# Wq loaded in twelve pieces of 16 rows instead of two pieces of 128, and x in one piece instead of three

## The chip, the core and the metric

The kernel runs on one core of a Trainium2 chip. The core has a matrix engine (TensorE, in the profile PE, with PEld for its weight loads), a vector engine (VectorE, DVE), a scalar engine (ScalarE, ACT), a general engine (GpSimd, POOL) and a synchronisation engine (SyncE, SP), which here only issues transfers. Transfers between the chip's memory (HBM) and the on-chip memory of 128 partitions (SBUF) run on 16 DMA engines; SP and ACT each have a queue on them. The metric is the device time of one execution in microseconds (us), as a median of several runs. A profile is the record of one execution; its span runs from the first to the last instruction of the program and is a little shorter than the device time of that execution.

## What is computed

One step of decoding for 8 sequences (B = 8, one token each): a layer norm of x, attention over a window of the last 2048 positions of a cache, and a gate from a small feed-forward unit. All arrays are bf16; D = 512, 32 query heads that share 8 key and value heads, head size 128, F = 1792.

```python
xn = layernorm(x)                                  # x: [8, 1, 512]
q = (xn @ wq).reshape(8, 1, 32, 128)               # wq: [512, 4096]
k, v = k_cache[:, :, -2048:, :], v_cache[:, :, -2048:, :]   # [8, 8, 2048, 128]; each serves 4 query heads
p = softmax(q . k * 128 ** -0.5)
s = (p . v).reshape(8, 1, 4096) @ wo               # wo: [4096, 512]
h = sigmoid(xn @ w_gate) * (xn @ w_up)             # [512, 1792] each
g = silu(h @ w_down)                               # [1792, 512]
out = x + s * g
```

Of 81 MB that are read, the windows of the K and V caches are 32 MB each in binary units, Wq and Wo 4 MB each, and the three matrices of the feed-forward unit 1.75 MB each.

## The kernel before

The order of the work is written out by hand. All large loads go through one function, `load` (its issue is L116), which issues on SP's queue; the transfers of that queue run in the order of their issues. The list `loads` fixes this order: after Wq the eight K tiles and sixteen V tiles, interleaved by their due slots, then the matrices of the feed-forward unit and Wo at the end.

Wq, the K tiles, and the weights of the end share a ring of three buffers (`kring`, 32 KB or less in each partition); the V tiles have a ring of four. Wq takes the first buffer of `kring`, the first two K tiles the other two. The third K tile can be issued only when the q projection has read Wq (the entry `(4, 0)` in `k_order`, released behind `q_projection`). `issue_loads` runs after each slot of the main loop and issues what has become possible.

In SBUF, row p of `wq_sb` holds rows 4p to 4p + 3 of Wq (the index `kt` is 0 to 3), that is 16,384 elements or 32 KB of contiguous memory. Before, two loads of 128 rows bring it: the first 4096 columns (kt = 0, 8 KB in each partition), then the other 12,288 (24 KB in each).

x is [8, 512]. It comes through ACT's queue (L126) in three pieces of columns 0 to 255, 256 to 383 and 384 to 511. L244 to L257 on VectorE and ScalarE normalise it, L267 on TensorE transposes it, L285 writes `xnT_sb`. The q projection (L405) then runs 32 matmuls: for each of two groups of heads and each kt, four matmuls with 32 columns of output partitions each. Every matmul reads all 128 partitions of `wq_sb` for its kt. `q_out` copies the result and lays it out in `qz_sb` (L419 to L436).

The main loop goes by slots. In each, VectorE transposes a quarter of the columns of a half K tile in place (`k_turn`, L464), TensorE makes scores four slots later (`qk`, L479), and later in the loop come the softmax, its transposes and the products with V (`pv`, L609). Behind the loop stand the last products, the feed-forward unit's output, and the product with Wo (L723), which takes Wo's six loads as they land. L734 and L736 combine, L738 stores.

In the compiled program a transfer takes one of eight completion semaphores in turn. An issue that reuses a semaphore waits until the transfer that had it eight places before has landed. Before the change, x and Wq take five (three and two); after it thirteen (one and twelve), so that the later transfers keep the same semaphores.

Of the kernel before, what the change touches and what calls it, by code (L numbers as in the profile page):

```python
# [10 lines left out]
def kernel(  # L11
# [13 lines left out]
    nc = tc.nc  # L25
    P = 128
# [53 lines left out]
    NSUM = 4  # L80
    NCOL = 2
    DC = D // NCOL
    WQ0 = 4096

    bf16 = mybir.dt.bfloat16
    f32 = mybir.dt.float32
# [26 lines left out]
    def load(dst, src, q=None):  # L113
        if q is None:
            q = nc.sync
        q.dma_start(out=dst, in_=src)  # L116
# [5 lines left out]
        return vring.tile(shape, bf16, name=name, tag="vring", align_bytes=ALIGN)  # L122

    x_bf = work.tile([B, D], bf16, name="x_bf")
    for c0, c1 in ((0, 2), (2, 3), (3, 4)):
        nc.scalar.dma_start(  # L126
            out=x_bf[:, P * c0 : P * c1],
            in_=A_x.flatten_outer_dims()[:, P * c0 : P * c1],
        )

    wq_sb = k_tile([P, KT, Hq * Dh], "wq_sb")
    wq_rows = A_wq.rearrange("(p kt) n -> p (kt n)", kt=KT)
    wq_flat = wq_sb[:].rearrange("p kt n -> p (kt n)")
    load(wq_flat[:, :WQ0], wq_rows[:, :WQ0])
    load(wq_flat[:, WQ0:], wq_rows[:, WQ0:])

    k_tiles = {}
    v_tiles = {}
# [77 lines left out]
    def issue_loads():  # L216
# [36 lines left out]
        out=rstd[:], in_=mv[:, 1:2], func=AF.Sqrt, bias=eps_t[:], scale=1.0  # L253
# [4 lines left out]
        out=xn_bf[:],  # L258
# [7 lines left out]
    for kt in range(KT):  # L266
        nc.tensor.transpose(  # L267
            out=xnT_ps[:, kt, :], in_=xn_bf[:B, kt::KT], identity=ident[:B, :B]
        )
    x2_ps = psum1.tile([NCOL * 32, DC], f32, name="x2_ps", tag="misc")  # L270
    for c in range(NCOL):
# [18 lines left out]
        out=HR[:],  # L290
        in_=ident[:].rearrange("m (h q r) -> m h r q", q=NQ, r=rep),
# [6 lines left out]
        out=Qm[:],  # L298
        in_=ident[:].rearrange("m (h q r) -> m q h r", q=NQ, r=rep),
# [6 lines left out]
        out=Hm[:],  # L306
        in_=ident[:].rearrange("p (a gl) -> p gl a", gl=GL),
# [6 lines left out]
    for j in range(GL):  # L314
        for gg in range(NG):
            g = NG * gg + j // 2
            nc.gpsimd.tensor_copy(
                out=spread[:, gg, j % 2, :, j], in_=ident[:, 32 * g : 32 * g + PP]
# [5 lines left out]
        out=rows_of[:],  # L324
        in_=ident[:].rearrange("p (a m) -> p m a", m=w),
# [5 lines left out]
        out=Sel[:], in_=rows_of[:].rearrange("p (g c r) -> p c g r", g=GL, c=NCH)  # L331
# [5 lines left out]
    for gg in range(NG):  # L337
        rows = slice(32 * gg, 32 * (gg + 1))
        cols = slice(NE * GL * rep * gg, NE * GL * rep * (gg + 1))
        for e in range(NE):  # L340
            nc.gpsimd.tensor_copy(
                out=pick[rows, e, cols].rearrange("p (h d) -> p h d", d=NE)[:, :, e],
                in_=ident[rows, 32 * gg : 32 * gg + GL * rep],
# [325 lines left out]
    for t in range(PV_LAG + NSLOT):  # L669
# [18 lines left out]
        if u >= NJ and u % NJ == 0:  # L688
            i = u // NJ - 1
# [47 lines left out]
    for c in range(NCOL):  # L737
        queues[c].dma_start(  # L738
            out=out.flatten_outer_dims()[:, DC * c : DC * (c + 1)],
            in_=y_bf[32 * c : 32 * c + B, :],  # L740
# [31 lines left out]
```

## Time and profile before

| | us |
|---|---|
| median of 3 runs | 197.32 (197.01 to 197.46) |
| the profiled execution | 197.11 |
| its span | 195.3 |
| TensorE busy (matmuls) | 102.8 |
| VectorE busy | 105.4 |
| ScalarE busy | 30.8 |
| GpSimd busy | 4.6 |
| mean rate of transfer over the span | 415 GB/s |

The page of the profile names the busy time of each engine, shows the span in 40 slices (a digit is the busy share in tenths), lists the transfer queues and their packets, and follows the chain of work that ended last back from the end. Further views are: the chain in order of time; a timeline of instructions; a table of stretches, with each engine's busy time and count, the clock granted to TensorE, the mean busy share of the DMA engines, and the rate in GB/s; and the instructions of one line of code, with the shortest, median and longest of them. A short stretch counts a packet of a transfer in the stretch where it begins, so its rate and share can lie above or below the true one.

### The profile page before, as it was taken

What the parts mean: (1) busy time and instruction counts of PE and PEld (TensorE: products, weight loads), DVE (VectorE), ACT (ScalarE), POOL (GpSimd) and SP (SyncE); (2) the same over time, 40 slices, a digit from 0 to 9 for tenths busy, and PEclk for the clock granted to TensorE, in tenths of its full rate; (3) what the DMA queues carried; (4) which work ended last, traced back from release to release, by engine and by line L of the source; (5) the groups of instructions that cost most, each with busy time, mean ns of one, the idle gap of its engine ahead of it and who ended that gap; (6) DMA issues with size and microseconds to landing.
All of it is one profiled execution on the core that took longest, in us unless ns stands there. A gap on an engine that the chain in (4) does not pass through costs nothing.

```text
span 195.3 us, 1888 instructions
## 1 busy us (share of the span) xinstructions
PE 102.8 (53%) x750; PEld 36.2 (19%) x750; DVE 105.4 (54%) x149; ACT 30.8 (16%) x69; POOL 4.6 (2%) x25
## 2 busy tenths in 40 slices
PE   0062014434323248403695989858943893577763
PEld 0020001101000012100121222322311131223451
DVE  0156499999899998899969726303100010040301
ACT  2025050000000084000011153511111114010100
POOL 8000000000000000000000000000000000000000
PEclk9999999999999999955588799988999798597999
DMA  6999999999999999999999999999999999999990
GB/s 251 449 450 436 456 429 429 429 429 421 429 429 429 429 429 429 393 429 463 429 419 429 433 423 429 431 433 429 426 433 433 429 426 426 437 426 429 419 399 34
DMA packets 5128, 81.14 MB, mean 415 GB/s; under 512 B 616, under 2 KB 768, under 8 KB 1152
## 3 DMA queue, kind: packets, MB, share of 16 engines
q1 hardware_dynamic: 5056, 81.01, 97.1%
q8 instruction: 6, 0.10, 0.2%
q10 hardware_dynamic: 64, 0.01, 0.0%
q14 instruction: 2, 0.02, 0.0%
HBM read 81.01 MB, written 0.01 MB: 415 GB/s over the span
## 4 chain that ended last, share of the span: by engine, by line
DMA 63%; DVE 21%; PE 12%; issue 1%; SPq 1%; ACT 1%; DVEq 0%
DMA k_sb<-in_A_k_cache_dram 31%; DVE k_sb L464 16%; DMA wgu_sb<-in_B_w_up_dram 13%; DMA wo_sb<-in_A_wo_dram 12%; DMA v_sb<-in_A_v_cache_dram 7%; PE acc_ps L609 5%; PE s_ps L479 3%; DVE pt_bf L527 2%; PE pT_ps L540 2%; PE o_ps L635 2%; SPq L116 1%; DVE mx L493 1%; DVE qz_sb L434 0%; DVE o_sb L644 0%; PE a_ps L723 0%
## 5 line engine op out<-in xcount | busy, mean ns | idle before, releaser
L464 DVE STREAM_TRANSPOSE k_sb<-k_sb 128x1024 f32<-128x1024 f32 x64 | 73.7, 1210 | 6.5 <-DMA k_sb<-in_A_k_cache_dram 6.5
L479 PE MATMUL s_ps<-k_sb,qz_sb 128*32 128x512 bf16 x256 | 29.7, 563 | 54.1 <-DVE k_sb L464 48.3
L609 PE MATMUL acc_ps<-v_sb,pT_sb 128*64 128x512 bf16 x256 | 39.6, 443 | 10.7 <-DMA v_sb<-in_A_v_cache_dram 10.6
L644 DVE TENSOR_TENSOR o_sb<-o_ps,rden 16x512 bf16<-16x512 f32 (+2 forms) x6 | 3.0, 504 | 47.5 <-PE o_ps L635 47.5
L479 PEld LDWEIGHTS <-qz_sb 128*32 128x32 bf16 x256 | 8.5, 115 | 78.5 <-issue 55.3
L623 ACT COPY acc_sb<-acc_ps 128x512 f32<-128x512 f32 x16 | 9.4, 585 | 84.7 <-PE acc_ps L609 84.7
L609 PEld LDWEIGHTS <-pT_sb 128*64 128x64 bf16 x256 | 13.3, 120 | 31.3 <-DMA v_sb<-in_A_v_cache_dram 14.5
L635 PE MATMUL o_ps<-acc_sb,Sel 128*16 128x512 f32 (+2 forms) x48 | 16.0, 478 | 3.4 <-ACT acc_sb L623 3.4
L561 DVE TENSOR_SCALAR pT_sb<-pc_bf,Hm 128x1024 bf16<-128x1024 bf16 x16 | 6.6, 477 | 6.8 <-PE acc_ps L609 6.7
L507 ACT ACT_TABLE_LOAD x1 | 1.3, 1283 | 39.9 <-DVE nm L501 39.9
L635 PEld LDWEIGHTS o_ps<-acc_sb,Sel 128*16 128x16 f32 x48 | 4.5, 103 | 15.1 <-issue 7.8
L493 DVE TENSOR_REDUCE mx<-s_ps 128x1 f32<-128x512 f32 x8 | 5.3, 662 | 3.2 <-PE s_ps L479 3.2
L540 PE MATMUL pT_ps<-pt_bf,spread 128*128 128x512 bf16 x16 | 6.0, 501 | 1.4 <-DVE pt_bf L527 0.7
L267 PE MATMUL xnT_ps<-ident,xn_bf 8*128 8x8 bf16 x4 | 0.3, 174 | 11.7 <-DVE xn_bf L257 11.7
L436 ACT COPY qz_sb<-qT_sb 32x32 bf16<-32x32 bf16 x20 | 4.8, 241 | 8.2 <-DVE qT_sb L424 7.9
L355 PE MATMUL d_ps<-wgu_sb,xnT_sb 128*32 128x448 bf16 x32 | 2.9, 502 | 5.4 <-DMA wgu_sb<-in_B_w_up_dram 3.0
L723 PE MATMUL a_ps<-wo_sb,o_sb 128*32 128x256 bf16 x64 | 4.5, 273 | 2.0 <-DMA wo_sb<-in_A_wo_dram 1.8
L507 ACT ACTIVATE p_bf<-s_ps,nm 128x512 bf16<-128x512 f32 x8 | 5.4, 684 | 0.0
L244 DVE CAST x_f<-x_bf 8x512 f32<-8x512 bf16 x1 | 0.4, 415 | 9.2 <-DMA x_bf<-in_A_x_dram 9.2
L548 ACT CAST pc_bf<-pT_ps 128x512 bf16<-128x512 f32 x8 | 4.5, 586 | 5.0 <-DVE pt_bf L527 2.8
L527 DVE STREAM_TRANSPOSE pt_bf<-p_bf 128x512 bf16<-128x512 bf16 x8 | 4.9, 668 | 0.0
L723 PEld LDWEIGHTS <-o_sb 128*32 128x32 bf16 x64 | 3.5, 96 | 3.1 <-issue 2.9
(59 smaller groups left out, 39.4 us busy)
## 6 DMA issues: line engine op xcount, KB each, us to landing
k_sb<-in_A_k_cache_dram SPq DMA_DIRECT2D x8, 4096.0 KB, 19.3
v_sb<-in_A_v_cache_dram SPq DMA_DIRECT2D x16, 2048.0 KB, 15.7
wq_sb<-in_A_wq_dram SPq DMA_DIRECT2D x1, 3072.0 KB, 11.5
wgu_sb<-in_B_w_gate_dram SPq DMA_DIRECT2D x1, 1792.0 KB
wgu_sb<-in_B_w_up_dram SPq DMA_DIRECT2D x1, 1792.0 KB, 24.7
wd_sb<-in_B_w_down_dram SPq DMA_DIRECT2D x1, 1792.0 KB
wo_sb<-in_A_wo_dram SPq DMA_DIRECT2D x1, 1536.0 KB
wo_sb<-in_A_wo_dram SPq DMA_DIRECT2D x1, 1152.0 KB, 33.8
```

What stands on the lines that cost most here:

```text
L436: nc.scalar.copy(out=out, in_=in_)
L464: nc.vector.transpose(out=kw, in_=kw)
L479: nc.tensor.matmul(s_tiles[i][32 * g : 32 * (g + 1), :], lhsT=qz_sb[:, hb, h, 2 * a + e, :], rhs=kT[:, :, a, h, :, e], start=(n == 0), sto ...
L493: nc.vector.reduce_max(out=mx_of[hb][:, kq : kq + 1], in_=s_tiles[i][:], axis=AX.X)
L507: nc.scalar.activation(out=p_bf[:, :, kq], in_=s_tiles.pop(NK * hb + kq)[:].rearrange("p (o c j) -> p c j o", o=2, j=NC), func=AF.Exp, bia ...
L527: nc.vector.transpose(out=pt[:, w * n : w * (n + 1)], in_=p_bf[:, w * n : w * (n + 1)])
L540: nc.tensor.matmul(pT_ps[:], lhsT=spread[:, gg, y].rearrange("p k g -> p (k g)"), rhs=pt[:, c, y, :], start=(y == 0), stop=(y == 1), skip_ ...
L561: nc.vector.tensor_scalar(out=pT_of[hb, gg][:, :, gl, :], in0=pc, scalar1=Hm[:, gl : gl + 1], scalar2=None, op0=ALU.mult,)
L609: nc.tensor.matmul(acc_tiles[i][w * c : w * (c + 1), :], lhsT=pT[:, GL * rep * ch : GL * rep * ch + w], rhs=v_tiles[i][:, ch : ch + NCH, : ...
L623: nc.scalar.copy(out=acc_sbs[i // NSUM][:, i % NSUM], in_=acc_tiles.pop(i)[:])
L635: nc.tensor.matmul(o_ps[rows, :n, :], lhsT=Sel[:, c].rearrange("p g r -> p (g r)"), rhs=acc_sb[:, :, Dh * c : Dh * (c + 1)], start=(c == 0 ...
L723: nc.tensor.matmul(a_ps[32 * c : 32 * (c + 1), :], lhsT=o2_sb[:, k, :], rhs=wo_parts[k][:, DC * c : DC * (c + 1)], start=(k == 0), stop=(k ...
```

## The change

The two loads of Wq become twelve. Set i (0 to 7) takes partitions i, i + 8, ..., i + 120, sixteen rows. Sets 0 to 3 come in two loads each, of 8192 columns (16 KB for each row); sets 4 to 7 come in one load each, of all 16,384 columns (32 KB). The bytes and where they end up are the same. x comes in one load. Nothing else is changed.

```diff
-    WQ0 = 4096
+    WQ0 = 8192
...
-    for c0, c1 in ((0, 2), (2, 3), (3, 4)):
-        nc.scalar.dma_start(
-            out=x_bf[:, P * c0 : P * c1],
-            in_=A_x.flatten_outer_dims()[:, P * c0 : P * c1],
-        )
+    nc.scalar.dma_start(out=x_bf[:], in_=A_x.flatten_outer_dims())
...
-    load(wq_flat[:, :WQ0], wq_rows[:, :WQ0])
-    load(wq_flat[:, WQ0:], wq_rows[:, WQ0:])
+    for i in range(P // 16):
+        for h in range(2 if i < 4 else 1):
+            c = slice(WQ0 * h, WQ0 * (h + 1)) if i < 4 else slice(0, 2 * WQ0)
+            load(wq_flat[i :: P // 16, c], wq_rows[i :: P // 16, c])
```

In the compiled order SP issues the twelve loads ahead of the first K load. The first seven wait for nothing; the eighth waits for x; the ninth to twelfth wait for the first four loads of Wq, and the first and second K loads for the fifth and sixth. The instructions of the other engines keep their order; the first matmul of the q projection and some of those behind it wait for all twelve loads instead of two.

## The prediction

> **What bounds the kernel now.** I read the page's DMA rows first, because the kernel moves 81 MB and does little arithmetic on it.
>
> ```profile
> DMA  6999999999999999999999999999999999999990
> GB/s 251 449 450 436 456 429 429 429 429 421 429 429 429 429 429 429 393 429 463 429 419 429 433 423 429 431 433 429 426 433 433 429 426 426 437 426 429 419 399 34
> q1 hardware_dynamic: 5056, 81.01, 97.1%
> ...
> q10 hardware_dynamic: 64, 0.01, 0.0%
> ```
>
> The transfers are busy in every slice but the first and the last, at about 429 GB/s whatever the slice computes. VectorE at 54% and TensorE at 53% have room. The loads of the SP queue (q1) fill 97.1% of what sixteen engines could do. The chain of waits, in order of time, says the same at both ends:
>
> ```profile
> 0.74 0.41 SPq L116
> ...
> 1.66 20.67 DMA k_sb<-in_A_k_cache_dram
> ...
> 168.08 23.52 DMA wo_sb<-in_A_wo_dram
> 191.60 0.04 issue
> ```
>
> The first K load is issued at 1.66 us and lands at 22.33, because 4 MB of Wq stand before it in the same queue; the last Wo load lands at 191.60 and 3.7 us of arithmetic and store follow. So the time is: start of the stream (about 1.7 us), 81 MB at the stream's rate, tail. A microsecond added to or taken from the stream anywhere is a microsecond of the kernel. The stretches (busy time of each engine, then granted clock, DMA share, GB/s) give the rates:
>
> ```profile
> 1.70:2.40 0.70, 0.00 (x0) 0.00 (x0) 0.00 (x0) 0.37 (x1) 0.70 (x2) 1.00 1.19 215
> 2.40:3.00 0.60, 0.00 (x0) 0.00 (x0) 0.00 (x0) 0.60 (x1) 0.54 (x5) 1.00 0.68 273
> ...
> 12.30:22.30 10.00, 3.58 (x32) 1.09 (x32) 3.92 (x16) 3.46 (x11) 0.00 (x0) 1.00 0.98 423
> 22.30:32.20 9.90, 1.90 (x16) 0.73 (x17) 9.76 (x13) 2.89 (x12) 0.00 (x0) 1.00 0.98 424
> 32.20:140.00 107.80, 62.51 (x424) 18.18 (x423) 83.74 (x103) 16.00 (x33) 0.00 (x0) 0.89 1.00 430
> 140.00:190.00 50.00, 32.29 (x252) 14.64 (x251) 4.98 (x8) 6.88 (x11) 0.00 (x0) 0.86 1.00 428
> ```
>
> The steady rate is 430 GB/s for rows of 32 KB (K), 16 KB (V) and 14 KB (gate, up, down) alike, 26.9 GB/s for each of sixteen engines; only the first 1.3 us are slow.
>
> **x in one piece.** In the timeline (start, length) x is late today:
>
> ```profile
> 9.17 0.41 DVE L244 CAST x_f<-x_bf 8x512 f32<-8x512 bf16 x1 [9.17 <-DMA x_bf<-in_A_x_dram]
> ...
> 12.21 3.68 PE L405 MATMUL q_ps<-wq_sb,xnT_sb 128*32 128x512 bf16 x32
> ...
> 22.36 2.37 DVE L464 STREAM_TRANSPOSE k_sb<-k_sb 128x1024 f32<-128x1024 f32 x2 [3.97 <-DMA k_sb<-in_A_k_cache_dram]
> ```
>
> One issue instead of three on ACT's queue removes two issues (326 ns is their median) and lets x land ahead of Wq, perhaps 6 us earlier. The normalisation from 9.17 to 12.21 moves forward with it. Worth nothing: the projection also needs all of Wq, and the first K load lands 6.4 us after the projection ends at 15.89. VectorE waits 3.97 us for it directly ahead of L464. Without that cover a late q would delay the first scores, but the last K load would still come on time.
>
> **Twelve issues for two.** From the views of the tiles `wq_sb` and `x_bf` (shortest, median, longest issue in ns):
>
> ```profile
> L116 SPq DMA_DIRECT2D wq_sb<-in_A_wq_dram x2: 407/408/408, 0.7 to 1.2; - x2
> ...
> L126 ACTq DMA_DIRECT2D x_bf<-in_A_x_dram x3: 278/326/592, 0.7 to 1.7; - x3
> ```
>
> A 16-row issue is not in the trace; the nearest rows are 278 to 592 ns (8 rows, ACT) and 408 ns (128 rows, SP). I take 0.4 us, plus 0.06 between issues. A half set is 0.26 MB, 0.61 us at 430 GB/s; a whole one 1.22 us. Twelve issues feed the stream faster than it drains, even at 0.59. In the compiled order the first seven issues wait for nothing; the eighth waits for x's landing, the ninth to twelfth for the first four Wq loads, the first two K loads for the fifth and sixth. Each waits for a load seven or eight places ahead, so the queue still holds about 4 us of data. Behind these waiting issues stand the K loads, wanted only when Wq is through. Cost: 0. The third K load still waits for the projection to release Wq's buffer, with two K loads (19 us) queued as cover.
>
> **Ten more loads in the stream.** Each must end on every engine. From 140 to 190 us the queue issues eleven loads and the stream makes 428 GB/s instead of 430: 0.23 us, some 0.02 us a load, so +0.2 us for ten (bounds 0 and 0.4).
>
> **The start.** From 1.7 to 3.0 us some 0.31 MB moved where 430 GB/s would move 0.56: 0.57 us lost. One row for each engine in the first load may start all of them together. With an issue 0.13 us shorter (278 for 408) the gain is at most 0.7; it may be 0. I take -0.2.
>
> **Which sixteen partitions are written at a time.** This term decides. Before, each engine carries one row at a time out of 128, and the hardware chooses which engine has which rows; 430 GB/s shows that those sixteen concurrent rows don't hinder each other. In the change set i fixes them: partitions i, i+8, ..., i+120, for all engines at once, with the same residue for 0.5 MB. Nothing in the trace has such a destination. If writes go through paths that belong to neighbourhoods of partitions, one path feeding one engine's rate, then neighbourhoods of eight leave every row its own path (Wq at 430 GB/s: 4.194 MB / 430 = 9.75 us, cost 0). Neighbourhoods of four leave every second path unused: two engines on each, 215 GB/s, 19.5 us, +9.75. Sets 0 to 3 would meet on one half of the paths, sets 4 to 7 on the other, in that order, so nothing evens out. The ends are 0 and +9.75; the slowest big load of the trace, Wq's first (1 MB in 4.6 us from issue to landing, 228 GB/s, latency included), lies near the slow end, if for another reason. I take +9.75: a full rate that doesn't depend on the row length looks like a fixed path width, and the edit takes from the hardware the choice that kept those paths apart.
>
> [...]
>
> **Sum.** 0 (x, issues) + 0.2 (ends of loads) - 0.2 (start) + 9.75 = +9.75 us. On the profiled execution, 197.11 us with a span of 195.3 and 1.8 us around it, this gives 206.9 and a span of 205.1. The median of the runs is 197.32, 0.2 above; I forecast 206.9.
>
> **Rivals.**
> - *No meeting of writes, a shorter start.* The rows keep their paths and the first slice alone changes: -0.7 to 0 with +0.2 for the ends of loads. At its best -0.5, 196.6; in the middle -0.15, 197.0. It decides from the point where the start returns more than 0.2 us. For it: the 0.57 us really lost, and no slow destination anywhere in this trace. Against it: no load here has a strided destination either. Faster if over half of the lost start comes back.
> - *SP becomes the bound.* A waiting issue comes too late and leaves a hole of the length from first issue to first byte, 0.74 to 1.70, 0.96 us; one hole gives 198.1, all five Wq issues with a wait 201.9. For it: those waits are new. Against it: each wait is for a load seven or eight places ahead.
> - *The loads don't spread.* A 16-row load uses only 8 engines: also 215 GB/s and 206.9, but with engines idle (four engines: +29 us). Against it: the packets. The SP queue has 35 loads of 128 rows and a store of 8; one packet for each row and one end for each engine make 35 x (128 + 16) + 8 + 8 = 5056, as the page counts, and ACT's four transfers of 8 rows make 4 x (8 + 8) = 64. So 128 rows go to sixteen engines and 8 rows to eight. For it: no load of 16 rows was seen.
>
> **Chances.** Meeting writes 0.62 (own range 205.4 to 207.5: the cost may fall short of the half by a tenth, -1.0, with -0.5 from start and ends of loads; or these add 0.4 and the median's offset 0.2); no meeting 0.28; SP the bound 0.08; too few engines 0.02. The range must reach to the second case to hold 8 in 10: 196.6 to 207.5. A difference under 0.2% (0.4 us) can't be told from none here. Of the 0.28, 0.15 is faster, 0.10 the same, 0.03 slower; the other cases are slower: 0.15, 0.10, 0.75.
>
> **What would show it.** In the stretches from 3 to 20 us: meeting writes give about 215 GB/s with a DMA share still near 1 (packets last longer), the first K load landing at 32 us instead of 22.3, and everything after that unchanged but 9.75 us later. Too few engines: the same GB/s with a share near 0.5. SP the bound: 430 GB/s with holes, and issues of L116 directly ahead of them. No meeting: about 430 GB/s from 2.5 us on, the K load at 21.8 to 22.5. x should be cast near 3 us and the projection start with Wq's last landing in each case. I am wrong if the first K load lands before 31 us.

## The result, and the profile after

The changed kernel takes 207.54 us (median of four runs, 207.35 to 207.57) against 197.38 us before: 1.0516 times as long, with a 95% interval of 1.0502 to 1.0530. The forecast was 206.9 with a range that ended at 207.5. The loss lies where the forecast put it, in Wq's loads at half the rate (210 GB/s from 12 to 22 us; before, 432 from 3 to 12), and one small term of the sum had the wrong sign. The medians differ by 10.16 us. The profiled execution took 207.57 us, 10.46 more than the one before, which was a short one of its kernel (197.11).

The page's transfer rows after the change: busy share and rate in 40 slices, then SP's queue q1 (packets, MB, share of sixteen engines):

```profile
DMA  6999899999999999999999999999999999999990
GB/s 154 204 255 204 306 433 471 420 408 433 463 420 408 439 465 420 408 423 430 468 408 420 433 423 436 423 435 427 439 420 439 423 433 435 431 427 420 430 399 33
q1 hardware_dynamic: 5152, 81.01, 97.0%
```

The first row looks like the one of before: the engines are as busy as ever. The second row doesn't: the first four slices, 20 us, move about half as much. Engines that stay busy and move half the bytes should have longer packets. The trace keeps the start and length of each packet (the packet records below), and they say so: the 64 packets of 32 KB of Wq took 2.54 us each at the median, the packets of 32 KB of K 1.21. The packets of q1 are 96 more than before: ten more loads with sixteen ends each, less 64 rows that are no longer cut in two.

The stretches (busy times of the engines, granted clock, DMA share, GB/s) put numbers on it:

```profile
1.75:2.00 0.25, 0.00 (x0) 0.00 (x0) 0.00 (x0) 0.25 (x1) 0.25 (x1) 1.00 0.04 8
2.10:2.30 0.20, 0.00 (x0) 0.00 (x0) 0.05 (x1) 0.20 (x1) 0.20 (x2) 1.00 2.86 819
3.00:12.00 9.00, 0.61 (x6) 0.31 (x6) 2.54 (x12) 0.66 (x2) 2.53 (x15) 1.00 1.10 229
12.00:22.00 10.00, 0.00 (x0) 0.00 (x0) 0.00 (x0) 0.00 (x0) 0.00 (x0) 1.00 0.98 210
22.00:32.00 10.00, 3.61 (x32) 1.27 (x32) 3.10 (x11) 3.10 (x10) 0.00 (x0) 1.00 0.94 396
42.00:150.00 108.00, 62.74 (x424) 18.14 (x423) 84.53 (x104) 16.19 (x33) 0.00 (x0) 0.89 1.00 429
```

From 12 to 22 us, 210 GB/s at a DMA share of 0.98; later 429 at 1.00, as before. The first two lines show the start: nothing of Wq begins between 1.75 and 2.00 us, and ten of its packets begin between 2.10 and 2.30. The same two stretches of the kernel before:

```profile
1.75:2.00 0.25, 0.00 (x0) 0.00 (x0) 0.00 (x0) 0.00 (x0) 0.25 (x1) 1.00 2.36 395
2.10:2.30 0.20, 0.00 (x0) 0.00 (x0) 0.00 (x0) 0.20 (x1) 0.20 (x2) 1.00 0.76 164
```

There the stream begins before 2.00 us. The changed stream starts some 0.4 us later: in the packet records Wq's first packet begins at 1.77 us before and at 2.15 after. In the timeline (start and length of a group; in brackets the idle time before it; line numbers are two lower than before) all of this arrives at the first scores:

```profile
2.25 0.47 DVE L242 CAST x_f<-x_bf 8x512 f32<-8x512 bf16 x1 [2.25 <-DMA x_bf<-in_A_x_dram]
...
23.80 3.61 PE L403 MATMUL q_ps<-wq_sb,xnT_sb 128*32 128x512 bf16 x32 [18.37 <-DMA wq_sb<-in_A_wq_dram]
...
32.95 2.37 DVE L462 STREAM_TRANSPOSE k_sb<-k_sb 128x1024 f32<-128x1024 f32 x2 [3.06 <-DMA k_sb<-in_A_k_cache_dram]
```

x is cast at 2.25 us instead of 9.17, and that buys nothing: TensorE then waits 18.37 us for Wq. The first K tile lands 10.6 us later than before (32.93 us against 22.33). In the chain of waits at the end, the last load of Wo ends at 202.07 us instead of 191.60, 10.47 later, and the tail has its old length:

```profile
178.55 23.52 DMA wo_sb<-in_A_wo_dram
202.07 0.04 issue
```

### The profile page after: what moved, and what is told of

It is laid out like the page before. It is cut to its first block, busy times and chain, and to the rows that moved or that the text cites. A ratio compares the mean times of both kernels' runs of the same rounds, so it can differ in the third digit from the quotient of the medians.

```text
span 205.8 us, 1899 instructions
## 1 busy us (share of the span) xinstructions
PE 101.7 (49%) x750; PEld 36.1 (18%) x750; DVE 105.5 (51%) x149; ACT 31.0 (15%) x69; POOL 4.9 (2%) x25
## 4 chain that ended last, share of the span: by engine, by line
DMA 64%; DVE 22%; PE 9%; SPq 2%; issue 1%; ACT 1%; ACTq 0%; DVEq 0%
DMA k_sb<-in_A_k_cache_dram 30%; DVE k_sb L462 17%; DMA wgu_sb<-in_B_w_up_dram 12%; DMA wo_sb<-in_A_wo_dram 11%; DMA v_sb<-in_A_v_cache_dram 7%; DMA wq_sb<-in_A_wq_dram 3%; PE acc_ps L607 3%; PE s_ps L477 2%; DVE pt_bf L525 2%; PE pT_ps L538 2%; PE o_ps L633 2%; SPq L116 2%; DVE mx L491 1%; DVE qz_sb L432 0%; DVE o_sb L642 0%
## 5 line engine op out<-in xcount | busy, mean ns | idle before, releaser
L607 PE MATMUL acc_ps<-v_sb,pT_sb 128*64 128x512 bf16 x256 | 38.5, 432 | 10.8 <-DMA v_sb<-in_A_v_cache_dram 10.7
L403 PE MATMUL q_ps<-wq_sb,xnT_sb 128*32 128x512 bf16 x32 | 3.6, 630 | 18.4 <-DMA wq_sb<-in_A_wq_dram 18.4
L422 DVE STREAM_TRANSPOSE qT_sb<-q_sb 128x512 bf16<-128x512 bf16 x2 | 1.4, 690 | 20.0 <-ACT q_sb L417 20.0
L403 PEld LDWEIGHTS <-xnT_sb 128*32 128x32 bf16 x32 | 1.3, 139 | 20.1 <-issue 20.1
```

The costliest lines, as they stand in the source:

```text
L403: nc.tensor.matmul(q_ps[gg][32 * gl : 32 * (gl + 1), :], lhsT=xnT_sb[:, kt, :], rhs=wq_sb[:, kt, h0 : h0 + HW], start=(kt == 0), stop=(kt ...
L607: nc.tensor.matmul(acc_tiles[i][w * c : w * (c + 1), :], lhsT=pT[:, GL * rep * ch : GL * rep * ch + w], rhs=v_tiles[i][:, ch : ch + NCH, : ...
```

## The experiments

Theory A is the prediction's: rows of one load that end up in partitions of the same write path share the rate of one engine, and four neighbouring partitions share a path. The paths, and the rows that meet on one, are the theory's: the records show the time of packets and the rate of stretches, and no run shows a path. Rivals: a stride is slow in itself (B), the number of loads or issues costs the time (C), and, for the later runs, that an engine is slow on any path but its own (D), that one waiting row holds up rows on other paths too (E), or that the limit is one of sixteen engines together (F). The edits replace the loop over Wq's loads in the changed kernel. Ratios are to the kernel before, run on the same chip.

**1. Sixteen neighbours.**

```diff
-            load(wq_flat[i :: P // 16, c], wq_rows[i :: P // 16, c])
+            load(wq_flat[16 * i : 16 * (i + 1), c], wq_rows[16 * i : 16 * (i + 1), c])
```

> Set i takes sixteen neighbouring partitions (16i to 16i+15) instead of each eighth one; loads, sizes, order and issues as in the changed kernel. Theory A (rows of one set meet on shared write paths, one path for four neighbours): sixteen rows now meet on four paths, so Wq runs at a quarter of 430 GB/s, 107 GB/s, 39 us instead of 19.5; about 227 us in all. Rival B (a stride of eight rows is slow in itself, at the source or the destination): the rows are contiguous, so the loss goes, about 198 us. Rival C (the number of loads or of their issues costs the time): the same as the changed kernel, 207.5.

Measured: 223.01 us, ratio 1.1314 (1.1292 to 1.1336). B and C fall: the stride is gone and the loss grows from 10 to 26 us. The stretches:

```profile
1.75:2.00 0.25, 0.00 (x0) 0.00 (x0) 0.00 (x0) 0.25 (x1) 0.25 (x1) 1.00 3.21 725
...
3.00:20.00 17.00, 0.61 (x6) 0.31 (x6) 2.82 (x13) 0.66 (x2) 2.70 (x16) 1.00 1.19 133
20.00:37.00 17.00, 0.00 (x0) 0.00 (x0) 0.00 (x0) 0.00 (x0) 0.00 (x0) 1.00 0.82 93
```

Over the two long stretches the mean is 113 GB/s, a quarter of 430 within 6%. The total is 4 us below the 227 expected. The first line tells a second thing: these sixteen-row loads start before 2.00 us, like the kernel before.

**2. The source made contiguous, the destination left as it was.**

```diff
-            load(wq_flat[i :: P // 16, c], wq_rows[i :: P // 16, c])
+            load(wq_flat[i :: P // 16, c], wq_rows[16 * i : 16 * (i + 1), c])
```

> The destination of each set stays each eighth partition; its source rows are sixteen neighbours of Wq, one contiguous stretch of memory (rows of Wq so land in other partitions than x's, and q is computed from a permuted Wq). Theory A (destination partitions decide): 207.5 us as in the changed kernel, 215 GB/s while Wq is loaded. Rival B (the stride of 256 KB between the rows of the source decides): about 198 us.

Measured: 207.41 us, 1.0518 (1.0502 to 1.0534), the changed kernel's own ratio (1.0516), with 206 GB/s from 12 to 22 us. The stride of the source has no part in it.

**3. Twelve loads by columns.**

```diff
+    CW = WQ0 // 8
+    for n in range(12):
+        c = slice(CW * n, CW * (n + 1)) if n < 8 else slice(2 * CW * (n - 4), 2 * CW * (n - 3))
+        load(wq_flat[:, c], wq_rows[:, c])
```

> Twelve loads of the same bytes in the same order (eight of 256 KB, four of 512 KB), x in one piece, but each load covers all 128 partitions and a stretch of columns (2 KB or 4 KB a row). Theory A: the meeting of rows is gone, Wq at nearly 430 GB/s; what is left of the loss is the ends of ten more loads (0.2 us), the shorter rows and a start that is later by the issue: 197.3 to 198.6 us. Rival C (twelve loads or their issues cost it): about 207 us. The start tells a second thing: if the first Wq byte comes 0.4 us later than before here too, it is x and the number of issues; if not, the 16-row form.

Measured: 199.12 us, 1.0091 (1.0076 to 1.0106). The large loss is gone with twelve loads of the same bytes, so C falls again. It is 0.5 us above the expected range: from 3 to 12 us the stream moves 351 GB/s, where the kernel before moves 432.

```profile
3.00:12.00 9.00, 3.01 (x18) 0.75 (x19) 2.54 (x12) 0.66 (x2) 2.53 (x15) 1.00 1.02 351
```

Rows of 2 and 4 KB, or the waits of its issues for earlier loads, are the two candidates. Waits would leave engines idle, and the DMA share is 1.02; that speaks for the short rows, which were not tried by themselves. The start is not late here: the first packet begins at 1.76 us, so neither x in one piece nor the number of issues delays it.

**4. x in one piece alone.**

```diff
+    for n in range(4):
+        c = slice(WQ0 // 2 * n, WQ0 // 2 * (n + 1))
+        load(wq_flat[:, c], wq_rows[:, c])
```

> x in one piece alone, with Wq in four loads of 128 rows and 8 KB a row (one x and four Wq loads, so that later transfers keep their semaphores). By the sum in the prediction x in one piece is worth nothing: 197.2 to 197.6 us, same as before, although x lands near 2 us instead of 9. Rival: x's three pieces between Wq's packets cost the stream something, or the early projection helps: below 196.9 us.

Measured: 197.42 us, 1.0011 (1.0002 to 1.0021). x is cast at 2.23 us, as in the changed kernel, and the time is that of before within 0.2%. The run also cuts Wq in four; rows of 8 KB keep 427 GB/s from 3 to 12 us.

**5. A stride of seven.**

```diff
+        rows = slice(i, i + 106, 7) if i < 7 else slice(112, 128)
...
-            load(wq_flat[i :: P // 16, c], wq_rows[i :: P // 16, c])
+            load(wq_flat[rows, c], wq_rows[rows, c])
```

> Again twelve loads of 16 rows, but set i (0 to 6) takes partitions i, i+7, ..., i+105, and the last load the sixteen neighbours 112 to 127. [...] With the later start of a strided load (0.4 us) that is about 202.5 us, and in the stretch of the first eleven loads over 350 GB/s. Rival B (any 16-row load, or any stride over partitions, runs at half rate): Wq over 19.5 us, 207.5 us or more.

Measured: 206.50 us, 1.0476 (1.0460 to 1.0491). The expectation failed:

```profile
3.00:8.00 5.00, 0.61 (x6) 0.30 (x6) 2.55 (x12) 0.66 (x2) 2.53 (x15) 1.00 1.07 252
8.00:11.00 3.00, 0.00 (x0) 0.00 (x0) 0.00 (x0) 0.00 (x0) 0.00 (x0) 1.00 1.18 339
```

From 3 to 8 us the stream moves 252 GB/s and from 8 to 11 us 339, under the 350 expected. It is not half rate (215) for any stride either.

**6 and 7. Thirty-two rows, and sixty-four.**

```diff
+    for i in range(4):                                        # 32 rows
+        load(wq_flat[i::4, :], wq_rows[i::4, :])
...
+    for i in range(2):                                        # 64 rows
+        for h in range(2):
+            c = slice(WQ0 * h, WQ0 * (h + 1))
+            load(wq_flat[i::2, c], wq_rows[i::2, c])
```

> Four loads of 32 rows (each fourth partition, 32 KB a row), x in one piece. [...] If the hardware gives each engine the rows of its own path, as it must do for 128 rows, Wq runs at 430 GB/s: 197.6 to 198 us. If it cuts the 32 rows into sixteen runs of two in order (engine e: partitions i+8e and i+8e+4), all engines write one half of the paths first and then the other: 215 GB/s, about 207.5 us.

> Two sets of 64 rows (each second partition), each in two loads of 16 KB a row, x in one piece. The same question as with 32 rows: 197.6 to 198 us if each engine gets rows of its own path, about 207.5 us if the rows are cut into sixteen runs in order (engine e: partitions i+8e, +2, +4, +6: two rows on one half of the paths, then two on the other).

Measured: 197.92 us, 1.0038 (1.0023 to 1.0053), and 197.70 us, 1.0027 (1.0015 to 1.0039). Both run at about the full rate: from 3 to 12 us 411 and 437 GB/s, where the kernel before moves 432. The stretches of the run with 32 rows:

```profile
1.75:2.00 0.25, 0.00 (x0) 0.00 (x0) 0.00 (x0) 0.25 (x1) 0.25 (x1) 1.00 0.04 8
2.10:2.30 0.20, 0.00 (x0) 0.00 (x0) 0.09 (x1) 0.20 (x1) 0.20 (x2) 1.00 5.23 1475
3.00:12.00 9.00, 0.61 (x6) 0.31 (x6) 2.54 (x12) 0.66 (x2) 2.53 (x15) 1.00 0.96 411
```

411 GB/s with a stride over partitions: loads of 32 rows don't lose the half that loads of sixteen lose. But the first byte is as late as in the changed kernel (2.10 and 2.09 us). These two runs so show the price of the strided start without the halved rate: 0.75 and 0.53 us over the kernel before on their own chip, against 0.2 for x in one piece with loads of 128 rows (run 4); by the difference the start itself costs some 0.3 to 0.6 us, an estimate.

**8. Sets 4 to 7 on ACT's queue.**

```diff
-            load(wq_flat[i :: P // 16, c], wq_rows[i :: P // 16, c])
+            load(wq_flat[i :: P // 16, c], wq_rows[i :: P // 16, c], queues[i // 4])
```

> Sets 0 to 3 stay on SP's queue, sets 4 to 7 go through ACT's, so that each engine has rows of both halves of the paths waiting at the same time. Theory A allows anything from 197.7 us (two engines of a pair always on different halves) to 207.9 us (always on the same). If they fall into step, as the same start suggests, it stays near 207.5; a time below 203 us would show that the halves can be used at once. Rival C (number of loads): 207.5 us.

Measured: 206.48 us (206.32 to 209.4), 1.0507 (1.0438 to 1.0577). Little or nothing is gained by offering the engines rows of sets 0 to 3 and of sets 4 to 7 at once: from 3 to 22 us the profile, which is of the longest of the four runs, has 231 GB/s at a DMA share of 1.01.

**9. Eight rows, each fourth partition.**

```diff
+    for s in range(16):
+        r0 = 32 * (s // 4) + s % 4
+        rows = slice(r0, r0 + 29, 4)
+        for h in range(2 if s % 8 < 2 else 1):
+            c = slice(WQ0 * h, WQ0 * (h + 1)) if s % 8 < 2 else slice(0, 2 * WQ0)
+            load(wq_flat[rows, c], wq_rows[rows, c])
```

> [...] First the eight sets of partitions 0 to 63, then the eight of 64 to 127; 32 KB a row, some in halves. [...] Theory A as the prediction put it (only rows that meet on a path slow each other): each engine keeps 26.9 GB/s, 215 GB/s in all, the same in both halves; Wq 19.5 us, about 207.5 us. Theory D (an engine has a path of its own, and writing through another engine's is slow, whether or not rows meet): the rates of the two halves differ, and at least one is well under 215; over 210 us.

Measured: 213.19 us, 1.0806 (1.0696 to 1.0916). By the total it would be D. The stretches say something else:

```profile
3.00:12.00 9.00, 0.61 (x6) 0.30 (x6) 2.54 (x12) 0.66 (x2) 2.53 (x15) 1.00 0.49 175
12.00:18.00 6.00, 0.00 (x0) 0.00 (x0) 0.00 (x0) 0.00 (x0) 0.00 (x0) 1.00 0.51 218
18.00:28.00 10.00, 0.00 (x0) 0.00 (x0) 0.00 (x0) 0.00 (x0) 0.00 (x0) 1.00 0.98 233
```

A share of 0.5 of sixteen engines is that of eight at work, whose full rate is 8 times 26.9, 215 GB/s. From 12 to 18 us they move 218 GB/s. By the bytes moved they pass from the sets of partitions 0 to 63 to those of 64 to 127 at about 14 us, so both halves reach this rate, and D falls. The first K load is issued at 17.82 us; from 18 to 28 us the share is 0.98, that of all sixteen engines, and together they move 233 GB/s. So eight engines alone had their full rate, and sixteen have half of theirs. That the K rows then meet Wq's rows on the same paths is A's reading, and wasn't tried by itself. The 175 GB/s of the first stretch is less than the 215 that A expects, by which no two rows of a set meet, and no run shows why.

**10 and 11. Eight rows, each fifth and each eighth partition.**

Against the loop of run 9; in the run with each fifth, the four sets that come in halves are the first four.

```diff
-        r0 = 32 * (s // 4) + s % 4
-        rows = slice(r0, r0 + 29, 4)
+        r0 = 40 * (s // 5) + s % 5                                          # each fifth
+        rows = slice(r0, r0 + 36, 5) if s < 15 else slice(120, 128)
...
+        r0 = 64 * (s // 8) + s % 8                                          # each eighth
+        rows = slice(r0, r0 + 57, 8)
```

> Loads of 8 rows, each fifth partition (sets of 40 partitions, the last load partitions 120 to 127). [...] Theory A with independent paths: six engines at full rate, two at half; Wq about 34 us on the slowest engine because the pair is mostly the same two engines, 221 us, and packets of 16 KB of two kinds, near 0.61 and 1.22 us. Theory E (a row that waits for its path holds up the others too, as the run with a stride of seven suggests): all packets between, none at the full rate, like there. Theory D: as for the run with 8 rows and a stride of four.

> [...] Theories A and E: half rate for every engine, 107 GB/s, Wq 39 us, about 227 us. Rival F (the limit is on sixteen engines together, not on a path): the eight engines keep 215 GB/s, 207.5 us.

Measured: 223.15 us, 1.1311 (1.1263 to 1.1360), and 232.96 us, 1.1808 (1.1774 to 1.1843). The stretches ahead of the first K load, each fifth partition and then each eighth:

```profile
3.00:8.00 5.00, 0.62 (x6) 0.31 (x6) 2.54 (x12) 0.66 (x2) 2.53 (x15) 1.00 0.48 144
8.00:13.00 5.00, 0.00 (x0) 0.00 (x0) 0.00 (x0) 0.00 (x0) 0.00 (x0) 1.00 0.51 177
13.00:18.00 5.00, 0.00 (x0) 0.00 (x0) 0.00 (x0) 0.00 (x0) 0.00 (x0) 1.00 0.52 216
```

```profile
5.00:20.00 15.00, 0.43 (x6) 0.12 (x3) 1.14 (x6) 0.36 (x1) 0.62 (x4) 1.00 0.55 114
20.00:27.00 7.00, 0.00 (x0) 0.00 (x0) 0.00 (x0) 0.00 (x0) 0.00 (x0) 1.00 0.55 112
```

In the run with each eighth partition eight engines (a share of 0.55) move 112 GB/s, half of the 218 that eight engines move in run 9 with each fourth, and near the 107 of A and E: F falls, since the rate halves with half the engines too.

Each fifth partition: six engines at the full rate and two at half, as expected, would be 7/8 of 215, 188 GB/s. The stretches have 144 and 177, then 216. That two rows of each set slow each other, from which the 221 us comes, is shown by no run: by the bytes moved, the five sets of partitions 40 to 79 fill most of the stretch from 13 to 18 us, and there the rate is the full one of eight.

Ahead of them the rate is below 188, as in run 9 it is below 215 at that time (175). So this run doesn't show that six engines run freely beside two that don't. Of the 64 packets of 16 KB, all in its first four sets, 20 took less than 0.65 us (0.61 is the full rate); with six of eight engines at the full rate 48 would. The others lie anywhere from 0.65 to 1.35 us.

## Why the prediction was right, and where it was wrong

**What bounds the kernel: right.** The stream's delay at the first K tile, 10.60 us, comes out at the end as 10.46.

**Sixteen strided rows at half the rate: right, within 0.2 us.** The term was 9.75 us, from half of 430 GB/s. Of the 10.46 us that the profiled pair differs by, the later start takes about 0.4; what is left for the halved rate and the ends of the loads is 10.06, where the prediction had 9.75 + 0.2. Runs 1, 2 and 11 show that the destination's partitions decide it (207.41 us with the source contiguous), that sixteen neighbours have a quarter of the rate (113 GB/s), and that the halving is the same with half the engines (112 against 218). The choice between four neighbours and eight was a judgement all the same: a full rate that doesn't depend on the row length, the reason given, doesn't tell the two apart.

Four neighbours on a path, with a path for each such group, would also not be enough for the halving: sixteen rows at a stride of eight fall into sixteen different groups of four. No run shows how many paths there are or which partitions would share one, so the counts of rows on paths, here and in the expectations, are not shown. In their place the runs show a rate for each choice of rows: eight rows 4 apart 218 GB/s and eight rows 8 apart 112, on eight engines; sixteen rows 8 apart 210 and sixteen neighbours 113, on sixteen, where loads of 128 rows have 430.

**The start: wrong, and the step that failed.** "With an issue 0.13 us shorter (278 for 408) the gain is at most 0.7; it may be 0. I take -0.2." The bounds left out a loss, and the runs show one. The first piece of the chain after the change (start, length), and the instructions of Wq's tile (shortest, median and longest issue in ns):

```profile
0.74 0.63 SPq L116
```

```profile
L116 SPq DMA_DIRECT2D wq_sb<-in_A_wq_dram x12: 493/588/627, 0.7 to 8.4; - x12
```

A sixteen-row issue with a stride takes 588 ns, not 400, and the first one 0.63 us where the chain of before has 0.41; the first byte comes about 0.4 us later. It isn't the sixteen rows: with sixteen neighbours (run 1) the median is 410 and the start is that of before. It isn't the source: run 2 has a contiguous source and 588. It is the stride over the destination's partitions, and with the halved rate gone (runs 6 and 7) it costs 0.75 and 0.53 us in all, the 0.2 of run 4 included. With +0.4 in place of -0.2 the sum is 10.35 us and the time 207.5, the one measured. The agreement is a little better than it deserves: the sum starts from the profiled 197.11, and against the medians, which moved by 10.16, 10.35 is 0.2 too much.

**The issues: right that they cost nothing, by a cover that was narrower than it looked.** 588 ns with the 0.04 us that the chain has between two issues is 0.63 us, more than the 0.61 us that a half set would take at full rate. The issues were hidden because the data took twice as long; at the full rate those of the half sets would have been a little slower than their data.

**x in one piece: right.** Worth nothing, by run 4, within the 0.2 us that this run is over the kernel before. **The ends of ten more loads:** 0.2 us was taken, and no run shows them alone. **SP as the bound and too few engines: right to be small.** The DMA share of 0.98 at 210 GB/s excludes both, since either would leave engines idle.

**What stays open.** Run 5. The 202.5 us and the 350 GB/s expected of it come from a count of rows on paths that no run shows; 252 and then 339 GB/s were measured, and in the packet records none of the 128 packets of 16 KB took less than 0.66 us, where 0.61 is the full rate. Theory E, a waiting row that holds up the others, would explain that. Run 10 doesn't exclude E, nor bear it out: 20 of 64 packets ran at about the full rate, and fewer than the expectation gives. Engines that fall out of step, so that rows of different sets slow each other, may have a part in both; no run tries it. The rates so are measured for neighbours and for strides of four and eight, and no count here gives those of strides of five and seven.

## What to carry to other kernels

When a kernel is bound by its stream of loads, look at which partitions a load covers before its size: here a DMA share of 0.98 at 210 GB/s, half the rate of before, was the sign of packets that lasted twice as long (2.54 us against 1.21). It doesn't prove by itself that the partitions are the cause, since run 3, whose loads cover all 128 partitions in short rows, has a share of 1.02 at 351 GB/s. Cut a large load by columns into rows that stay long (8 KB in run 4, 427 GB/s), or not at all; if it must be cut by rows, sixteen rows gave half (each eighth partition, 210 GB/s) or a quarter of the rate (neighbours, 113) where 32 rows, each fourth partition, gave 411 GB/s. When a sum bounds an operation that the trace doesn't show, leave room for a loss as well as for a gain, even where the new form is smaller: it was the 0.6 us between -0.2 and +0.4 that put the result just past the end of the range.

## What the runs showed of the hardware that was not expected

A load of Wq with a stride over partitions is slower to issue than one of 128 rows without (588 ns against 408); loads of eight rows take 623 ns for each fourth partition and 563 for each eighth. A stride isn't the only thing that lengthens an issue: the K loads of 128 rows without one take 535 ns.

Loads of 32 and 64 strided rows ran at 411 and 437 GB/s from 3 to 12 us, 197.92 and 197.70 us in all. The expectation had two cases, rows dealt to the engines in order (about 207.5 us) and not (197.6 to 198 us), and the times are those of the second. How the rows are dealt to the engines no record shows. They could be dealt in order after all if engines fell out of step; run 8, where rows of sets 0 to 3 and 4 to 7 were waiting together and the rate stayed at 231 GB/s, speaks against that, but no run tries it alone.

And x, in one piece of 8 KB, is ready at 2.25 us where three pieces, which begin between packets of Wq, were ready at 9.17. In the packet records of the kernel before, the three pieces begin at 1.7, 5.6 and 7.4 us: it is the second and the third that wait.
